# Order of two output products at the end of a segment, in a segmented-attention and GeGLU kernel

## The chip, the cores and the metric

The kernel runs on one core of one Trainium2 chip. The metric is the device time of one execution in microseconds. An engine is named by its usual letters: PE is TensorE (matmuls; PEld are its weight loads), DVE is VectorE, ACT is ScalarE, POOL is GpSimd, SP is SyncE. A DMA is issued by SP, ACT or POOL and then runs on the core's 16 DMA engines.

## The reference

Two branches work on the same `x` (2048 rows of 1024) and are mixed by a gate. Branch A is an attention over 64 segments of 32 rows with a memory of 8 rows that each segment hands to the next, so that the segments are a recurrence. Branch B is a GeGLU feed-forward network.

```
for s in range(n_seg):                      # 64 segments, one after the other
    h = concat([mem, x[s*32:(s+1)*32]])     # 40 rows
    q, k, v = h Wq, h Wk, h Wv              # 32 heads of 128
    p = softmax(where(mask, q k^T * scale, -1e9))
    o = (p v) Wo                            # 40 rows of 1024
    mem = o[:8]                             # memory of the next segment
    outs.append(o[8:])
g = sigmoid((x * gate_w).sum(-1))
b = (gelu(x w_gate) * (x w_up)) w_down
return g * concat(outs) + (1 - g) * b
```

## The kernel before

**Branch B comes first** (up to about 600 us of the span). Its product, already multiplied by (1 - g), goes to a scratch tensor `b_scr` in HBM. Gates lie in SBUF in `gseg` and `ge`.

**Then the 64 segments run, one Python iteration of `for s in range(NSEG)` each.** The weights of branch A do not all fit in SBUF. What is missing, 19 blocks of 512 KB a segment, is read again in every segment from `w_scr` into `ring`, which has room for five blocks. SP issues a block's load (L614) as soon as TensorE has used up the two ring slots that it goes into; this is the weight stream below.

**Rows of a segment.** The 8 first rows of each segment are not needed by the recurrence in the same way as the others, so four segments' first rows (4 x 8 = 32) are put together and computed once for four segments ("ext" jobs, function `ext_jobs`). The segment itself works on 24 rows of `x` and 8 rows of memory. The accumulated output of the segment stands in PSUM bank `PB[B_O]`; that of the 32 first rows in `PB[B_X]`, which is used in every fourth segment only: in the segments with `"o"` in `jobs`, s = 3, 7, 11, ... 63.

**A segment in order.** Projections q, k, q, v, k, v for two halves of the heads (`emit_P`, matmuls of line L951, into two banks that take turns, `acc`), transposes (`emit_T`, L996 and L1004), scores and softmax (`emit_S`), its transposes (`emit_PT`), the product with v (`emit_PV`, whose L1081 also writes the first rows' part into `oe`), and the output projection (`emit_O`, L1114). Ext jobs (L836 and L1097) are put between.

**The end of a segment** is the place that the change touches. ScalarE copies `PB[B_O]` to `rows` (L1338), TensorE transposes it (L1350), and VectorE copies the memory columns into `hT` (L1356). With that the next segment's first projection, q, can start. Its second one, k, writes the bank that `B_O` names, since the two banks take turns; so its first matmul waits until L1362 has read it.

- L1362, VectorE: `bo = gate * PB[B_O] + bo`, the segment's own output product. `bo` was loaded with the rows of `b_scr` (`load_b`, L734).
- L1368: four stores of `bo` to the output, on POOL's queue; in the last segment two on SP's and two on ACT's.
- `out_first` (L1146 to L1164), only where `"o"` is in `jobs`: L1154 on ScalarE scales the upper half of `PB[B_X]`, L1156 on VectorE multiplies the lower half and adds the upper, L1159 on VectorE adds branch B's rows (`rowsx`), and L1162 issues two stores from `oe`, on POOL's queue; in the last segment on SP's and ACT's.
- Behind it POOL's queue goes on with the next segment's loads of `vt` (`load_vte`, L720), of `qkst` (L708) and of `bo` (L734).

**What sets the order.** The program is written as a list of operations. Each engine runs its own in the order in which the list has them. Waits are semaphores that `_Sched` derives from the keys which an operation reads and writes (`r=`, `w=`). So where an operation stands in the list decides what it is queued behind on its engine. A PSUM bank that two engines read is read by one after the other (`_Sched.op`, L45).

The loop's end as it stands, with the functions that it calls:

Of the kernel before, what the change touches and what calls it, by code (L numbers as in the profile page):

```python
# [26 lines left out]
class _Sched:  # L27
# [10 lines left out]
    def op(self, eng, mk, r=(), w=(), dsem=None):  # L38
        o = _Op(eng, mk, dsem)
        deps = []  # L40
        if eng == "pool" and dsem is None:
            w = [*w, ("pool",)]
        for k in r:
            deps += self.w.get(k, ())
            if k[0] == "P":  # L45
                deps += [x for x in self.r.get(k, ()) if x.eng != eng]
        for k in w:
            deps += self.w.get(k, ())
            deps += self.r.get(k, ())
        for k in r:  # L50
            self.r.setdefault(k, []).append(o)
        for k in w:
            self.w[k] = [o]
            self.r[k] = []
        seen = set()
        for d in deps:
            if d is o or id(d) in seen:
                continue
            seen.add(id(d))
            if d.eng == eng and d.dsem is None and (eng == "pe" or eng == "sp"):  # L60
                continue
            o.deps.append(d)
            d.sig = True
        self.ops.append(o)
        return o
# [63 lines left out]
def bass_gated_mix__memory_aug_recurrent_mem_tr__geglu_ffn__prompt_kernel(  # L129
# [38 lines left out]
    with ExitStack() as es:  # L168
# [50 lines left out]
        def P(i):  # L219
            return ("P", i)  # L220

        g = _Sched()
        op = g.op
# [501 lines left out]
        def rows_of(s):  # L725
            n = SEG if s + 1 < NSEG else NR
            v = of[s * SEG + EXT:s * SEG + EXT + n, :]
            return [(v[:, q * 256:(q + 1) * 256], bo[32 * q:32 * q + n, :]) for q in range(4)]
# [12 lines left out]
        def first_rows(t, j, q):  # L741
            return t.rearrange("(g s r) d -> g s r d", s=GR, r=SEG)[j, :, 0:EXT, q * 512:(q + 1) * 512]
# [52 lines left out]
        for s in range(NSEG):  # L795
# [350 lines left out]
            def out_first():  # L1146
                if "o" not in jobs:
                    return
                j = jobs["o"]
                flat = [oe[z:z + 64, :, :].rearrange("p a b -> p (a b)") for z in (0, 64)]  # L1150
                sums, to = flat[0].bitcast(FP32), flat[1][:, 0:512]
                key = [("oe", y) for y in range(NO)]
                gk = [("gseg", "e%d%d" % (q, u)) for q in range(4) for u in range(GR)]
                op("act", lambda e: e.activation(sums, PB[B_X][64:128, :], ACTF.Copy, scale=ge[64:128, j:j + 1]),  # L1154
                   r=[P(B_X)] + gk, w=key)
                op("dve", lambda e: e.scalar_tensor_tensor(  # L1156
                    out=sums, in0=PB[B_X][0:64, :], scalar=ge[0:64, j:j + 1], in1=sums, op0=ALU.mult, op1=ALU.add),
                   r=[P(B_X)] + gk, w=key)
                op("dve", lambda e: e.tensor_tensor(out=to, in0=sums, in1=rowsx[0:64, :], op=ALU.add), r=RX, w=key)  # L1159
                for q in range(2):  # L1160
                    op(("sp", "act")[q] if last else "pool",
                       lambda e, q=q: e.dma_start(first_rows(of, j, q), to[32 * q:32 * q + 32, :]),  # L1162
                       r=key + [("out", x, y) for x in range(max(0, j * GR - 1), j * GR + GR - 1) for y in range(4)],
                       w=[("oute", j, q)], dsem="%s%d" % ("ende" if last else "oute", q))  # L1164
# [192 lines left out]
                back("act", ("q", 0, 4, 1), 1)  # L1357
            flush()
            last = s == NSEG - 1
            if not last:  # L1360
                out_first()
            op("dve", lambda e, s=s, B_O=B_O: e.scalar_tensor_tensor(  # L1362
                out=bo[:, :], in0=PB[B_O][:, 0:256], scalar=gseg[:, s:s + 1], in1=bo[:, :], op0=ALU.mult, op1=ALU.add),
               r=[P(B_O)] + [("gseg", "%s%d" % (k, q)) for k in "ab" for q in range(4)], w=[("bo", x) for x in range(4)])
            for put, bank in ends:
                put(bank)
            for x, (d, b) in enumerate(rows_of(s)):
                op(("sp", "act")[x % 2] if last else "pool", lambda e, d=d, b=b: e.dma_start(d, b),  # L1368
                   r=[("bo", x)], w=[("out", s, x)], dsem="%s%d" % ("end" if last else "out", x))
            if last:  # L1370
                out_first()
            if s > GR and s % GR == 2 and s // GR + 2 < NG:
                load_xe(s // GR + 2)

# [40 lines left out]
```

## Time and profile before

| what | us |
|---|---|
| median of 3 runs (2481.06 to 2482.62) | 2482.28 |
| the profiled execution | 2473.53 |
| its span, first to last instruction | 2471.4 |
| PE busy in the span | 2203.8 |
| DVE busy | 1186.5 |
| ACT busy | 940.9 |
| POOL busy | 634.9 |
| ring loads: 1216 of 512 KB, median from issue to landing | 6.3 |

The page of the profile shows one execution. Busy time is the sum of what an engine's instructions took; a chain of waits follows the end of the span back to what released it at each step; a group is all instructions of one line, engine and operation, with its busy time, the mean of one, and the idle time of the engine just before them with what ended it. A timeline lists instructions by start time. Busy times in stretches list each engine's busy time, the granted clock of TensorE, the DMA engines' busy share and what they moved. From about 645 us on, the span consists of the segments, of 27 to 33 us each.

### The profile page before, as it was taken

How to read it: one execution, taken by the hardware profiler on the slowest of the kernel's cores; microseconds unless marked ns; L12 is line 12 of the kernel's file. 1: busy time of each engine (PE TensorE's matmuls, PEld its weight loads, DVE VectorE, ACT ScalarE, POOL GpSimd, SP SyncE). 2: the span in 40 equal slices, each digit the busy share in tenths (PEclk: the TensorE clock that was granted, in tenths of full speed). 3: DMA queues.
4: the chain of work that ended last, by engine and by line, in shares of the span. 5: the costliest groups of instructions: out<-in, count | busy, mean ns of one | idle time of the engine just before them, and what ended most of it. 6: DMA issues, size and time to landing. Idle time of an engine off the chain costs nothing.

```text
span 2471.4 us, 83513 instructions
## 1 busy us (share of the span) xinstructions
PE 2203.8 (89%) x37171; PEld 1100.2 (45%) x37171; DVE 1186.5 (48%) x3451; ACT 940.9 (38%) x2212; POOL 634.9 (26%) x1132
## 2 busy tenths in 40 slices
PE   9999999999888888888888888888888888988877
PEld 4444444444444444444444444444444444444433
DVE  5626264451444455544454454455454445545444
ACT  4314132230434444444444444444444344444433
POOL 1010102102332223233323222332323232332222
PEclk9999999999999999999999999999999999999999
DMA  8727354468999999999999999999999999999998
GB/s 276 259 69 253 103 181 124 128 227 302 346 345 362 366 372 373 379 367 369 367 380 364 369 362 384 372 373 375 371 378 371 364 370 378 371 376 360 376 345 301
DMA packets 293167, 797.45 MB, mean 323 GB/s; under 512 B 48352, under 2 KB 112016, under 8 KB 292040
## 3 DMA queue, kind: packets, MB, share of 16 engines
q1 hardware_dynamic: 249308, 736.77, 80.8%
q0 software_dynamic: 43392, 55.30, 7.1%
q8 instruction: 291, 4.77, 0.8%
q14 instruction: 68, 0.56, 0.1%
q10 hardware_dynamic: 108, 0.06, 0.0%
HBM read 764.52 MB, written 37.22 MB: 324 GB/s over the span
## 4 chain that ended last, share of the span: by engine, by line
PE 54%; DMA 28%; DVE 10%; ACT 5%; issue 2%; POOL 0%; ACTq 0%; SPq 0%; DVEq 0%; POOLq 0%
DMA ring<-w_scr 27%; PE pbb L951 5%; PE pba L951 5%; PE pbc L836 5%; PE pbb L1114 3%; PE pba L1114 3%; PE pbe L1061 3%; PE pba L449 2%; PE pbd L449 2%; PE pbg L449 2%; PE pbf L449 2%; PE pbe L449 2%; PE pbh L449 2%; PE pbc L449 2%; PE pbb L449 2%
## 5 line engine op out<-in xcount | busy, mean ns | idle before, releaser
L951 PE MATMUL pbb<-arena,hT 128*32 128x512 bf16 x4416 | 337.7, 381 | 21.3 <-DVE bo L1362 21.3
L951 PE MATMUL pba<-arena,hT 128*32 128x512 bf16 x4416 | 347.8, 380 | 0.1
L720 POOL DMA_DIRECT2D vt<-v_scr x252 | 148.1, 592 | 383.4 <-PE pbf L1072 233.9
L1004 DVE COPY qk<-pbe 128x512 bf16<-128x512 bf16 x129 | 89.1, 691 | 321.9 <-PE pbe L996 315.5
L1044 ACT ACTIVATE pbd<-pbd 104x160 f32<-104x160 f32 x256 | 71.9, 281 | 437.1 <-DVE pbd L1042 437.1
L1066 DVE COPY ptb<-pbe 80x320 bf16<-80x320 bf16 x256 | 82.2, 321 | 263.3 <-PE pbe L1061 263.3
L951 PE MATMUL pba<-ring,hT 128*32 128x512 bf16 x1542 | 152.4, 384 | 34.7 <-DMA ring<-w_scr 33.3
L951 PE MATMUL pbb<-ring,hT 128*32 128x512 bf16 x1536 | 148.7, 385 | 34.9 <-DMA ring<-w_scr 33.3
L836 PE MATMUL pbc<-arena,xe 128*32 128x512 bf16 x2208 | 177.0, 385 | 0.7 <-ACT rowsx L850 0.5
L951 PEld LDWEIGHTS pbb<-arena,hT 128*32 128x32 bf16 x4416 | 109.6, 97 | 108.4 <-DVE bo L1362 28.7
L957 ACT ACTIVATE rows<-pba 128x512 bf16<-128x512 f32 x128 | 76.5, 598 | 211.0 <-PE pba L951 211.0
L1368 POOL DMA_DIRECT2D out_dram<-bo x252 | 125.8, 505 | 111.2 <-DVE bo L1362 111.0
L951 PEld LDWEIGHTS pba<-arena,hT 128*32 128x32 bf16 x4416 | 113.2, 97 | 90.8 <-issue 2.5
L957 ACT ACTIVATE rows<-pbb 128x512 bf16<-128x512 f32 x128 | 76.5, 598 | 186.8 <-PE pbb L951 186.8
L1051 DVE TENSOR_TENSOR pn<-pbd,rr 104x256 bf16<-104x256 f32 (+1 forms) x512 | 141.8, 318 | 8.7
L1061 PE MATMUL pbe<-ident,pn 104*80 104x104 bf16 x1024 | 95.5, 216 | 40.9 <-DVE pn L1051 14.2
L880 POOL DMA_DIRECT2D qk_scr<-rowsx x60 | 47.3, 789 | 329.5 <-DVE rowsx L877 329.5
L1114 PE MATMUL pba<-arena,oT 128*32 128x256 bf16 x2176 | 121.6, 281 | 10.2 <-ACT oT L1080 5.3
L1114 PE MATMUL pbb<-arena,oT 128*32 128x256 bf16 x2176 | 119.0, 277 | 11.7 <-ACT oT L1080 11.7
L1114 PE MATMUL pba<-ring,oT 128*32 128x256 bf16 x1792 | 107.0, 279 | 22.0 <-DMA ring<-w_scr 21.4
L1045 DVE TENSOR_REDUCE rs<-pbd 104x4 f32<-104x160 f32 x256 | 83.0, 324 | 88.9 <-ACT pbd L1044 88.9
L1061 PEld LDWEIGHTS pbe<-ident,pn 104*80 104x80 bf16 x1024 | 62.7, 117 | 122.8 <-issue 51.8
(262 smaller groups left out, 4369.2 us busy)
## 6 DMA issues: line engine op xcount, KB each, us to landing
ring<-w_scr SPq DMA_DIRECT2D x1216, 512.0 KB, 6.3
arena<-in_B_w_gate_dram SPq DMA_DIRECT2D x27, 1024.0 KB, 5.4
arena<-in_B_w_up_dram SPq DMA_DIRECT2D x27, 1024.0 KB, 7.8
qkst<-qk_scr POOLq DMA_DIRECT2D x126, 64.0 KB, 5.6
qk_scr<-rowsx POOLq DMA_DIRECT2D x60, 128.0 KB, 5.8
arena<-in_B_w_down_dram SPq DMA_DIRECT2D x7, 1024.0 KB, 11.8
arena<-in_A_Wk_dram SPq DMA_DIRECT2D x6, 1024.0 KB, 7.2
arena<-in_A_Wv_dram SPq DMA_DIRECT2D x6, 1024.0 KB, 10.3
```

The source lines that it names most:

```text
L449: ins = e.matmul(PB[bank][:, :], lhsT=wv[:, kc, col:col + 128], rhs=xb[:, kc, :], start=(kc == 0), stop=(kc == KC - 1))
L720: op("pool", lambda e: e.dma_start(vt[2 * SEG:KEYS, par, :], v_scr[s // GR, h, 2 * par:2 * par + 2, s % GR, :, :]), r=[("vscr", s // GR, h ...
L836: ins = e.matmul(PB[B_X][32 * gq:32 * gq + 32, :], lhsT=xe[:, us[-1], :], rhs=us[gq // 2][0][gq % 2], start=(n == 0), stop=(n == KC - 1), ...
L951: ins = e.matmul(PB[bank][32 * gq:32 * gq + 32, :], lhsT=hT[:, kc, :], rhs=us[gq // 2][0][gq % 2], start=(x == 0), stop=(x == KC - 1), ski ...
L957: op("act", lambda e: e.activation(rows[:, :], PB[bank][:, :], ACTF.Copy), r=[P(bank)], w=[("rows",)])
L1004: op("dve", lambda e: e.tensor_copy(qk[:, m, :, 0:SEG, :], src), r=[P(B_T)], w=[("qk", m)])
L1045: op("dve", lambda e: e.tensor_reduce(rsv, sv, AX.X, ALU.add), r=[P(B_S)], w=[("rs",)])
L1051: op("dve", lambda e, c0=c0, k0=k0, n=n: e.tensor_tensor(out=pn[0:104, :, c0:c0 + 2 * n].rearrange("p i (two c) -> p i two c", two=2), in0 ...
L1061: ins = e.transpose(PBV[B_PT][0:KEYS, 512 + i * 128:512 + i * 128 + 104], pn[0:104, i, :], ident[0:104, 0:104])
L1066: op("dve", lambda e: e.tensor_copy(ptb[0:KEYS, :, :, :], src), r=[P(B_PT)], w=[("ptb",)] + first)
L1114: ins = e.matmul(PB[B_O][32 * q:32 * q + 32, 0:256], lhsT=oT[:, o % 2, k, :], rhs=u[q // 2][:, (q % 2) * 256:(q % 2 + 1) * 256], start=(o ...
L1368: op(("sp", "act")[x % 2] if last else "pool", lambda e, d=d, b=b: e.dma_start(d, b), r=[("bo", x)], w=[("out", s, x)], dsem="%s%d" % ("en ...
```

## The change

The own product L1362 now comes right behind the memory copy in every segment, and `out_first` comes behind the own stores L1368 in every segment (in the last segment it stood there already). In the last segment all four own stores are issued by SP instead of two by SP and two by ACT; the two of `out_first` stay on SP and ACT.

```diff
             last = s == NSEG - 1
-            if not last:
-                out_first()
             op("dve", lambda e, s=s, B_O=B_O: e.scalar_tensor_tensor(
                 out=bo[:, :], in0=PB[B_O][:, 0:256], scalar=gseg[:, s:s + 1], in1=bo[:, :], op0=ALU.mult, op1=ALU.add),
                r=[P(B_O)] + [("gseg", "%s%d" % (k, q)) for k in "ab" for q in range(4)], w=[("bo", x) for x in range(4)])
             for put, bank in ends:
                 put(bank)
             for x, (d, b) in enumerate(rows_of(s)):
-                op(("sp", "act")[x % 2] if last else "pool", lambda e, d=d, b=b: e.dma_start(d, b),
+                op("sp" if last else "pool", lambda e, d=d, b=b: e.dma_start(d, b),
                    r=[("bo", x)], w=[("out", s, x)], dsem="%s%d" % ("end" if last else "out", x))
-            if last:
-                out_first()
+            out_first()
             if s > GR and s % GR == 2 and s // GR + 2 < NG:
                 load_xe(s // GR + 2)
```

## The prediction, made before the changed kernel ran

> **What bounds the kernel now.** I read the chain of waits first. It says which resource keeps ending last over the whole span:
>
> ```profile
> PE 54%; DMA 28%; DVE 10%; ACT 5%; issue 2%; POOL 0%; ACTq 0%; SPq 0%; DVEq 0%; POOLq 0%
> ```
>
> Nearly all of the DMA share is one transfer, the weight blocks of 512 KB that SP loads into `ring` (27% of the span). So TensorE and the weight stream share the bound: TensorE runs until the next block has not landed, and a block is only issued when TensorE has freed two slots. Next come the costliest groups, for the place that the change touches:
>
> ```profile
> L951 PE MATMUL pbb<-arena,hT 128*32 128x512 bf16 x4416 | 337.7, 381 | 21.3 <-DVE bo L1362 21.3
> ```
>
> TensorE stands idle for 21.3 us in front of projection matmuls until VectorE's L1362 has read the output bank. The view of line L1362 counts 15 such waits, so 1.42 us each. Fifteen is the number of segments with `"o"` in `jobs` that are not the last (3, 7, ... 59). The timeline around the end of segment 11, one of them, shows why (start, duration, engine, line):
>
> ```profile
> 965.87 0.19 DVE L1356 COPY hT<-pbe 128x64 bf16<-128x64 bf16 x1 [2.04 <-PE pbe L1350]
> 966.69 0.68 ACT L1154 ACTIVATE oe<-pbc,gseg 64x512 f32<-64x512 f32 x1
> 967.41 0.74 DVE L1156 SCALAR_TENSOR_TENSOR oe<-pbc,gseg,oe 64x512 f32<-64x512 f32 x1 [1.35 <-ACT oe L1154]
> 968.28 0.69 DVE L1159 TENSOR_TENSOR oe<-oe,rowsx 64x512 bf16<-64x512 f32 x1
> 969.00 0.48 DVE L1362 SCALAR_TENSOR_TENSOR bo<-pbb,gseg,bo 128x256 bf16<-128x256 f32 x1
> 969.54 0.61 PE L951 MATMUL pbb<-arena,hT 128*32 128x512 bf16 x8 [1.52 <-DVE bo L1362]
> ```
>
> The memory copy L1356 ends at 966.06 and the next segment's q projection starts. VectorE then idles 1.35 us for ScalarE's L1154, does L1156 and L1159, and only then L1362, whose bank the k projection needs. At an ordinary boundary, the one of segment 12, nothing lies between the two:
>
> ```profile
> 995.29 0.19 DVE L1356 COPY hT<-pbe 128x64 bf16<-128x64 bf16 x1 [0.51 <-PE pbe L1350]
> 995.39 0.48 DVE L1362 SCALAR_TENSOR_TENSOR bo<-pba,gseg,bo 128x256 bf16<-128x256 f32 x1
> ```
>
> Last I read busy times in stretches, because the stall can only be won if the weight stream keeps up. These are the first 10 us behind the memory copy in segments 12 to 15; segment 12 has the stall. Columns: stretch, length, busy us of PE, PEld, DVE, ACT, POOL, granted clock, DMA share, GB/s.
>
> ```profile
> 966.10:976.10 10.00, 7.98 (x164) 3.63 (x164) 4.94 (x12) 3.29 (x7) 4.95 (x9) 1.00 0.96 325
> 995.50:1005.50 10.00, 9.58 (x200) 4.60 (x204) 2.95 (x8) 3.12 (x7) 3.74 (x7) 1.00 1.03 395
> 1023.10:1033.10 10.00, 9.32 (x196) 4.36 (x196) 2.81 (x9) 2.52 (x6) 4.06 (x8) 1.00 1.00 364
> 1051.80:1061.80 10.00, 8.09 (x160) 3.52 (x160) 3.01 (x8) 2.63 (x6) 4.85 (x9) 1.00 1.03 393
> ```
>
> The same four as whole segments:
>
> ```profile
> 966.10:995.50 29.40, 24.76 (x536) 12.69 (x536) 15.30 (x50) 12.73 (x31) 9.08 (x16) 1.00 0.98 355
> 995.50:1023.10 27.60, 24.53 (x536) 12.71 (x536) 13.71 (x48) 11.91 (x30) 7.95 (x14) 1.00 1.01 383
> 1023.10:1051.80 28.70, 25.44 (x552) 12.96 (x552) 14.67 (x53) 12.16 (x30) 8.16 (x14) 1.00 1.00 378
> 1051.80:1080.40 28.60, 24.96 (x520) 12.63 (x520) 12.94 (x43) 11.11 (x28) 9.45 (x17) 1.00 1.02 382
> ```
>
> A stalled segment is longer (over segments 4 to 62 the time from copy to copy averages 29.6 us, against 28.4, 28.6 and 28.8 for the three that follow it) though TensorE works no more, and the DMA engines move fewer bytes a second in it.
>
> **The change, part by part.**
>
> 1. L1362 moves ahead of `out_first` (15 boundaries). Its inputs are there: ScalarE's read of the same bank (L1338) precedes the transposes that feed L1356. So it starts at the copy's end, as at ordinary boundaries, and ends 0.5 us later instead of 3.4 us. It fits into VectorE's 1.35 us of idle time before L1156, so L1156 and L1159 stay where they are, ending 2.9 us behind the copy. If that idle time were gone, they would be 0.48 us later, and behind them the copy L1004 of the next q rows. That one starts 4.8 us behind the memory copy now (970.86) and would be wanted at about 3.3, so it has 0.4 us to spare and pays nothing. ScalarE's order does not change at these boundaries.
>
> 2. TensorE: the eight q steps end 1.95 us behind the copy, after the bank is free. The wait goes whole: at most 15 x 1.42 = 21.3 us.
>
> 3. How much of it the ring takes back. No row shows a first-rows boundary without the stall, so I bound it. Upper end: the whole 1.42 us. Lower end: segment 15, 10 us behind its copy, has no stall and still only 8.09 us of matmuls against 7.98 in stalled segment 12, with the same sort of work; it waits for blocks instead. Adding up TensorE's idle time ahead of `ring` matmuls gives 2.5 us in a segment of its kind and 1.1 in a stalled one, and 1.1 + 1.42 is 2.5 too: a gain of 0. Against that end: a stalled segment moves 29.4 x 355 = 10.4 MB, others 10.6 to 10.9 MB. At the other three's 381 GB/s it would be done in 27.4 us, 2.0 us sooner, so the stream has room for the whole stall. And part of its slow 325 GB/s is the stall's own doing: blocks whose slots the k projection frees are issued 1.5 us late and leave a hole. Segments of segment 14's kind wait 1.4 us for blocks on average; with that the stalled one would gain 1.42 + 1.1 - 1.4 = 1.1. I take **0.85 us**, between the midpoint 0.71 and 1.1: 15 x 0.85 = 12.75 us.
>
> By the Trainium skill (DMA: Bandwidth & Descriptors, Specifications) a core's share of HBM bandwidth is about 358 GB/s; a kernel already there could gain nothing from a shorter TensorE wait, and the sum would be 0.5 us. The trace does not agree with it as a ceiling: it has 395 GB/s for 10 us and whole slices at 384.
>
> 4. POOL's queue: the four stores of `bo` now come ahead of the two of `oe`. POOL issues a store in 0.50 us (4 in 2.02) and one of `oe` in 0.59. The stores go out 0.7 to 2.7 us behind the copy instead of 4.4 to 6.4, as at ordinary boundaries. Those of `oe` wait for L1159 (2.9) and go at about 3.2, as before. Behind them stand the two `vt` loads (L720), which gain some 2 us. The next writer of `oe`, L1081, and the next load of `bo`, L734, come over 9 us behind the copy, after the landing (5.4 and 4.5 us): cost 0. Without that cover each would cost its lateness to the part of the landing still open. The collision of these stores with the ring is a rival below.
>
> 5. The last segment. Here L1362 is already first; ScalarE's share of the stores goes to SP:
>
> ```profile
> 2462.23 0.75 SPq L1368 DMA_DIRECT2D out_dram<-bo  x2
> 2462.23 1.00 ACTq L1368 DMA_DIRECT2D out_dram<-bo  x2
> 2463.28 0.68 ACT L1154 ACTIVATE oe<-pbc,gseg 64x512 f32<-64x512 f32 x1 [2.62 <-PE pbc L1097]
> ```
>
> L1154 stands behind ScalarE's two issues; TensorE finished its bank at 2462.74. Without them it starts at about 2462.8, and L1156, L1159 and the last stores follow: **0.5 us**, once. SP issues 4 x 0.375 = 1.5 us, to 2463.7; its store of `oe` is due at 2465.1, so SP costs nothing. Without that cover, 0.75 us.
>
> Sum: 12.75 + 0.5 = 13.3 us. Against the profiled execution (2473.53 us, span 2471.4) that is 2460.2 and 2458.1. The median of the runs, 2482.28, lies 8.75 us above that execution; I take the gain from the median: **2469.0 us**. 0.2% of it, about what a measurement can tell from no change, is 5 us.
>
> **Rivals.**
> - **Whole stall won.** For: the stream's room of 2.0 us, the missing hole. Against: segment 15. 2482.3 - 21.3 - 0.5 = **2460.5 us**.
> - **The ring takes it all.** For: DMA shares of 0.96 to 1.03 everywhere, segment 15's first 10 us. Against: the bytes. Gain 0 to 0.3 a boundary: **2478 to 2482 us**.
> - **Slower: the earlier stores of `bo` collide with the blocks of the k and q projections.** At present they go out while TensorE has just been idle; after the change they go out 0.7 to 2.7 us behind the copy, when these blocks are in flight and TensorE runs without pause. At boundaries that have this now, ring waits reach 3.2 us in the worst segment. The price is the growth of ring waits over 1.1 us, and it decides from 1.42 us of growth on. At 3.2 the net is 3.2 - 1.1 - 1.42 = 0.7 us: 2482.3 + 15 x 0.7 - 0.5 = **2492 us**. Against: the stalled segment has the least other traffic.
> - That the change doesn't do what it says (L1362 held by something else, as at the one boundary of 15 where a late block already hides 1 us of the stall): no row speaks for it; it counts with the second.
>
> **How the numbers follow.** Forecast 0.53 (gain 5 to 18 us); whole stall 0.23; ring takes all 0.14; slower 0.10. Faster by over 0.2%: 0.53 + 0.23 + 0.03 of the second = 0.79; within 0.2%: 0.12; slower: 0.09. The likeliest's own range is 2464 to 2477. The range reaches to 2459 (the whole stall and a little of the hole) and to 2480, inside the second rival; outside lie the slower case, 0.1, and some 0.08 of the edges.
>
> **What would show it.** Right: L1362 ends 0.5 us behind L1356 at all boundaries; no TensorE wait on L1362; idle time ahead of `ring` matmuls grows by 15 x 0.57 = 8.5 us; the first 10 us of the 15 segments rise from about 8.0 us of matmuls and 325 GB/s to 360 or more; L1154 of the last segment starts 0.5 us behind its bank. Wrong: ring waits that grow by 20 us or more, a new wait of L1004 or of POOL's `vt` loads, or segments that follow growing longer by what these 15 lose.

## The result, and the profile after

The changed kernel takes 2459.39 us (median of 4 runs, 2455.58 to 2462.47); the kernel before takes 2482.09 us beside it. The ratio is 0.9908, with a 95% interval of 0.9891 to 0.9925: 22.7 us faster. The time lies in the stated range, but near its lower edge. Two repetitions further down give a smaller gain, 11 and 15 us.

The profiled execution of the changed kernel took 2462.47 us, 11.1 us less than the one of before, and its span is 2460.7 us. Its chain of waits, by engine and, the larger shares, by line:

```profile
PE 52%; DMA 32%; DVE 9%; ACT 4%; issue 2%; POOL 0%; SPq 0%; DVEq 0%; another core or an unknown queue 0%; POOLq 0%
DMA ring<-w_scr 30%; PE pba L951 6%; PE pbb L951 5%; PE pbc L836 5%; PE pbb L1114 3%; PE pba L1114 2%; PE pbe L1061 2%; PE pbg L449 2%; PE pbh L449 2%; PE pbf L449 2%; PE pbe L449 2%; PE pbe L996 2%; PE pba L449 2%; PE pbc L449 2%; PE pbd L449 2%
```

The weight stream's share rose from 27% to 30%. Of the costliest groups, the one that had 21.3 us of idle time before it, and two of the matmuls that read streamed blocks (busy us, mean ns, idle us and what ended it):

```profile
L951 PE MATMUL pbb<-arena,hT 128*32 128x512 bf16 x4416 | 339.9, 383 | 0.0
L951 PE MATMUL pba<-ring,hT 128*32 128x512 bf16 x1542 | 152.9, 385 | 36.5 <-DMA ring<-w_scr 35.3
L951 PE MATMUL pbb<-ring,hT 128*32 128x512 bf16 x1536 | 151.4, 387 | 36.7 <-DMA ring<-w_scr 35.1
```

The wait for the own product is gone entirely. The waits for blocks in the two lower groups were 33.3 us each before. The timeline at the end of segment 11, the boundary that the prediction showed (the own product is now L1360, its stores are L1366):

```profile
960.46 0.19 DVE L1356 COPY hT<-pbe 128x64 bf16<-128x64 bf16 x1 [2.04 <-PE pbe L1350]
960.57 0.48 DVE L1360 SCALAR_TENSOR_TENSOR bo<-pbb,gseg,bo 128x256 bf16<-128x256 f32 x1
962.00 0.74 DVE L1156 SCALAR_TENSOR_TENSOR oe<-pbc,gseg,oe 64x512 f32<-64x512 f32 x1 [0.96 <-ACT oe L1154]
962.88 0.69 DVE L1159 TENSOR_TENSOR oe<-oe,rowsx 64x512 bf16<-64x512 f32 x1
```

VectorE's order is the new one, and L1159 still ends 2.9 us behind the copy. TensorE and POOL in the same stretch:

```profile
962.44 0.60 PE L951 MATMUL pbb<-arena,hT 128*32 128x512 bf16 x8
962.88 0.91 PE L951 MATMUL pbb<-ring,hT 128*32 128x512 bf16 x8
...
961.34 2.01 POOL L1366 DMA_DIRECT2D out_dram<-bo  x4 [6.45 <-DVE bo L1360]
...
963.86 1.21 POOL L1162 DMA_DIRECT2D out_dram<-oe  x2 [0.52 <-DVE oe L1159]
...
965.06 1.14 POOL L720 DMA_DIRECT2D vt<-v_scr  x2
```

The k projection starts 1.8 us behind the copy (960.65) without a pause. It then meets its second streamed block: eight matmuls of `ring` take 0.91 us where they took 0.60. The `vt` loads go out 4.4 us behind the copy, 2 us sooner than before. The busy times of segment 12 in stretches, as in the prediction:

```profile
960.60:970.60 10.00, 8.71 (x176) 3.99 (x180) 5.60 (x15) 3.39 (x7) 4.92 (x9) 1.00 0.98 362
960.60:989.30 28.70, 25.06 (x536) 12.63 (x536) 15.20 (x51) 12.89 (x31) 9.05 (x16) 1.00 1.00 367
```

In the first 10 us, 0.73 us more of matmuls than before and 362 GB/s instead of 325; the segment is 28.7 us long instead of 29.4.

### The profile page after: what moved, and what is told of

Its sections match the earlier page's. It is cut to its first block, busy times and chain, and to the rows that moved or that the text cites. A ratio compares the mean times of both kernels' runs of the same rounds, so it can differ in the third digit from the quotient of the medians.

```text
span 2460.7 us, 83457 instructions
## 1 busy us (share of the span) xinstructions
PE 2204.1 (90%) x37115; PEld 1100.5 (45%) x37171; DVE 1185.1 (48%) x3451; ACT 941.3 (38%) x2212; POOL 634.8 (26%) x1132
## 4 chain that ended last, share of the span: by engine, by line
PE 52%; DMA 32%; DVE 9%; ACT 4%; issue 2%; POOL 0%; SPq 0%; DVEq 0%; another core or an unknown queue 0%; POOLq 0%
DMA ring<-w_scr 30%; PE pba L951 6%; PE pbb L951 5%; PE pbc L836 5%; PE pbb L1114 3%; PE pba L1114 2%; PE pbe L1061 2%; PE pbg L449 2%; PE pbh L449 2%; PE pbf L449 2%; PE pbe L449 2%; PE pbe L996 2%; PE pba L449 2%; PE pbc L449 2%; PE pbd L449 2%
## 5 line engine op out<-in xcount | busy, mean ns | idle before, releaser
L1366 POOL DMA_DIRECT2D out_dram<-bo x252 | 125.6, 506 | 224.2 <-DVE bo L1360 214.6
L1114 PE MATMUL pbb<-ring,oT 128*32 128x256 bf16 x1792 | 106.3, 277 | 14.8 <-DMA ring<-w_scr 14.5
```

The costliest lines, as they stand in the source:

```text
L1114: ins = e.matmul(PB[B_O][32 * q:32 * q + 32, 0:256], lhsT=oT[:, o % 2, k, :], rhs=u[q // 2][:, (q % 2) * 256:(q % 2 + 1) * 256], start=(o ...
L1366: op("sp" if last else "pool", lambda e, d=d, b=b: e.dma_start(d, b), r=[("bo", x)], w=[("out", s, x)], dsem="%s%d" % ("end" if last else ...
```

## The experiments

All were timed in five rounds beside the kernel before on the same chip.

**The two kernels again, and each part alone.** `before_again` and `after_again` are the two kernels as they stand. `bounds_only` is the changed kernel with the last segment's stores on SP and ACT as before; `last_only` is the kernel before with only those stores moved (`...` stands for the rest of a line):

```diff
-                op("sp" if last else "pool", lambda e, d=d, b=b: e.dma_start(d, b),       # bounds_only, from after
+                op(("sp", "act")[x % 2] if last else "pool", lambda e, d=d, b=b: e.dma_start(d, b),
-                op(("sp", "act")[x % 2] if last else "pool", lambda e, d=d, b=b: ...      # last_only, from before
+                op("sp" if last else "pool", lambda e, d=d, b=b: ...
```

> The kernel before, once more, as a measure of what two programs with the same text differ by, and for a second profile of it. Both theories: ratio to the kernel before 1.000, within 0.002. The second profile again has 15 waits of TensorE on L1362, 21 us in all.

> The changed kernel, once more. Theory A (forecast: the ring takes back some 0.57 us of each stall of 1.42 us): ratio 0.9947, 13 us faster. Theory B (the whole stall of 21.3 us is won, and 0.5 us at the end): ratio 0.9912, 22 us faster. If the ratio falls near 0.9955, as the two profiled executions have it (2473.53 and 2462.47 us), the first four timed runs overstated it.

> The own product first at the 15 boundaries; the last segment's stores stay on SP and ACT. Theory A: 12.8 us faster (0.9949). Theory B: 21.3 us faster (0.9914). Rival: much of the gain comes from the last segment, then this one lies over 2 us behind the changed kernel.

> Only the last segment's four stores on SP. Theories A and B: L1154 starts 0.5 us sooner behind TensorE, 0.5 us faster, which times cannot tell from no change (0.999 to 1.001). Rival: over 2 us faster.

| kernel | median us | ratio to before (2475.08 us) | 95% interval |
|---|---|---|---|
| before_again | 2473.18 | 0.9997 | 0.9969 to 1.0025 |
| after_again | 2460.69 | 0.9939 | 0.9911 to 0.9968 |
| bounds_only | 2465.84 | 0.9955 | 0.9928 to 0.9981 |
| last_only | 2473.41 | 0.9984 | 0.9960 to 1.0008 |

The gain of `after_again` is 15 us by its ratio (14.4 by the medians), between theory A and the first result and nearer to A. Its interval, 8 to 22 us, still holds theory B's 0.9912; that of `bounds_only` doesn't. `bounds_only` lies 5 us behind `after_again`, and over 2 us was my sign for a gain that comes from the last segment. The times can't settle that: the two intervals overlap, and `last_only` can't be told from no change. The timeline does: here is ScalarE's L1154 in `last_only`. In the kernel before it idled 2.62 us and started 0.5 us later.

```profile
2465.74 1.56 SPq L1368 DMA_DIRECT2D out_dram<-bo  x4
2466.30 0.69 ACT L1154 ACTIVATE oe<-pbc,gseg 64x512 f32<-64x512 f32 x1 [2.13 <-PE pbc L1097]
2468.61 0.75 SPq L1162 DMA_DIRECT2D out_dram<-oe  x1
```

From L1362's start to L1154's it is now 1.08 us instead of 1.56, as the prediction had it, and SP's four issues end 1.3 us before its next one. From L1362's start to the end of the span it is 9.69 us in the profile of before, 9.67 in that of `bounds_only`, and 9.18 in those of `last_only` and of the changed kernel. So the last segment gives 0.5 us and not 5, and the rest of the gain is at the 15 boundaries. A third time the changed kernel was run later, for the size:

> The changed kernel a third time, for the size of the gain. Theory A: 0.9935 to 0.996 (10 to 16 us). Theory B: 0.991 (22 us), as in the first four runs.

2460.42 us against 2471.79, ratio 0.9954 (0.9933 to 0.9976): 11 us, theory A. So the changed kernel's median hardly moves (2459.4, 2460.7, 2460.4), and what moved is the kernel before. Its four runs in the first comparison lay between 2481.1 and 2482.6; its 85 runs in the four later ones lie between 2460.0 and 2493.9, with medians of 2471.8 to 2476.4. The 24 runs of the two repetitions and these 85, taken together though they are from several chips, have means 14.2 us apart (about 3.5 either way): the forecast's 13.3 lies inside, the whole stall's 21.8 outside. Of the 85, 19 lie at 2481 us or above, so four such runs in a row are rare by chance alone; what held them there is not known. Because they lie close together, the first interval came out narrower than the spread of this kernel allows.

**Is it the ring that takes part of the gain?** In both kernels, every streamed block from the fifth segment on is cut to its first half (`half_...`) or its first three quarters (`three_quarter_...`, with 768 for 512):

```diff
+            if s >= 4:
+                op("sp", lambda e: e.dma_start(ring[:, sl:sl + wd, :].rearrange("p a b -> p (a b)")[:, 0:wd * 512], src[:, 0:wd * 512]),
+                   r=[("rp", u)], w=[("ring", y, x) for y in slots for x in range(2)], dsem=f"ring{sl}")
+                return
```

> The kernel before with every ring block from the fifth segment on cut to its first half (256 KB of 512 KB; the rest of the slot keeps older weights, so the output is another one). The weight stream no longer limits: nearly no waits of TensorE on ring blocks. The waits on L1362 stay, 15 of 1.5 us. Both theories: faster than the kernel before by its ring waits, some 1.5 us a segment, 60 to 100 us (0.96 to 0.975).

> The changed kernel with the same half blocks. With the ring out of the way, the gain over the half-block kernel before is the whole stall: 15 x 1.5 = 22 us. Theory A (the ring takes back some 40% in the kernel as it is): 22 us here against 13 to 15 there. Theory B (nothing is taken back): 22 us here and there. Rival C (the gain is limited by something other than the ring, VectorE or the later segments): here too only 13 to 15 us.

> The kernel before with ring blocks of 384 KB instead of 512 KB from the fifth segment on (the last quarter of each slot keeps older weights, so the output is another one). Theory A: ring waits mostly gone; some 20 us over the half-block kernel before at most: 2373 to 2395 us.

> The changed kernel with the same blocks of 384 KB. Theory A: what the ring takes back falls with the stream, so the gain over the three-quarter kernel before lies between the 13 to 15 us of the full stream and the 25.5 us of the half one, nearer the upper end: 20 to 25 us. Theory B: 25 us at every width. Rival C (the difference between 25.5 and 13 to 15 us is chance): no order, anything from 13 to 25.

`half_before` came out at 0.9586, a little faster than expected (0.96 to 0.975), `three_quarter_before` inside its range. The pairs:

| blocks | before's order, us | changed order, us | gain, us | ring wait per stalled segment, before and after |
|---|---|---|---|---|
| 512 KB (after_again, after_third) | 2475.08, 2471.79 | 2460.69, 2460.42 | 14.4, 11.4 | 1.1 and 1.5 |
| 384 KB | 2390.99 | 2379.52 | 11.5 | 0.06 and 0.65 |
| 256 KB | 2372.54 | 2347.06 | 25.5 | 0.00 and 0.01 |

The last column is the idle time of TensorE ahead of matmuls that read streamed blocks, averaged over the segments that follow a first-rows boundary, in one profile of each kernel. With full blocks it varies: 1.0 to 1.5 in three profiles of before's order, 1.4 to 1.7 in five of the changed one. The groups of the half-block pair, first before's order and then the changed one, show the whole stall going and nothing coming back:

```profile
L955 PE MATMUL pbb<-arena,hT 128*32 128x512 bf16 x4416 | 339.0, 383 | 22.9 <-DVE bo L1366 22.9
L955 PE MATMUL pbb<-ring,hT 128*32 128x512 bf16 x1536 | 147.7, 383 | 1.8 <-DMA ring<-w_scr 1.7
```

```profile
L955 PE MATMUL pbb<-arena,hT 128*32 128x512 bf16 x4416 | 338.2, 382 | 0.0
L955 PE MATMUL pbb<-ring,hT 128*32 128x512 bf16 x1536 | 147.3, 382 | 2.1 <-DMA ring<-w_scr 2.1
```

With the ring out of the way the change is worth 25.5 us, the 22.9 us of waits and a little more. That speaks for theory A: the whole stall comes off when the ring doesn't limit. Rival C, something other than the ring, falls. My expectation for three quarters was a miss: 11.5 us, not 20 to 25. The same groups of that pair, in the same order, show where it went:

```profile
L955 PE MATMUL pbb<-arena,hT 128*32 128x512 bf16 x4416 | 338.7, 382 | 22.9 <-DVE bo L1366 22.9
L955 PE MATMUL pbb<-ring,hT 128*32 128x512 bf16 x1536 | 147.7, 382 | 11.7 <-DMA ring<-w_scr 11.2
```

```profile
L955 PE MATMUL pbb<-arena,hT 128*32 128x512 bf16 x4416 | 339.2, 383 | 0.0
L955 PE MATMUL pbb<-ring,hT 128*32 128x512 bf16 x1536 | 148.2, 383 | 19.2 <-DMA ring<-w_scr 18.9
```

Before the change these segments had almost no ring waits (0.06 us), and after it 0.65. So the waits are not there because the stream as a whole is too slow; over 900 to 2200 us its DMA share (last column but one) is 0.91 in the 384 KB kernel of before, where it is 1.00 with full blocks and 0.69 with half:

```profile
900.00:2200.00 1300.00, 1156.15 (x25416) 610.83 (x25408) 669.75 (x2241) 567.21 (x1359) 413.12 (x725) 1.00 0.91 299
```

Nor is it full just there: in the 8 us behind the memory copy of these segments the share is 0.82 before the change and 0.85 after it. The waits come from single blocks. Following each block of the full-stream kernels through the trace (issue on SP, landing, first matmul that reads it; us behind the memory copy, mean over the segments 4, 8, ... 56) gives:

```
                       before                        after
block               issue   land   use   wait    issue   land   use   wait
3  (k, second)      -3.17   3.11   4.16  0.00    -3.20   2.96   3.00  0.38
4  (q, first)       -1.18   4.37   5.68  0.00    -1.17   4.27   4.57  0.03
5  (q, second)       0.72   6.05   6.64  0.04     0.72   5.94   5.99  0.36
6  (v, first)        1.48   7.34   8.24  0.00     1.38   7.33   7.52  0.02
7  (v, second)       4.36  10.03  10.12  0.45     2.68   9.19   9.23  0.28
11 (v, second half)  8.89  16.34  17.07  0.00     8.18  15.26  16.17  0.00
```

Blocks 3 to 6 are issued before the stall could hold anything back, so they land at the same time in both kernels, and TensorE, now 1.2 us earlier at block 3, runs into them. Block 7 is the first whose slots the stall held: it is issued 1.7 us sooner, but lands only 0.84 us sooner. From there on the segment is 0.9 us ahead. With 384 KB the waits after the change are at blocks 5, 6 and 7 (0.23, 0.11 and 0.25 us; before it 0.04 at block 7 alone), and block 7, there too issued 1.7 us sooner, lands no sooner at all (8.41 against 8.36 us). So an earlier issue isn't the whole of it: block 7 also takes longer in flight (5.75 against 3.99 us), and no run here shows why.

**What a stall costs elsewhere.** In the changed kernel, a stall is put in at the 45 ordinary boundaries (`idle` is a new buffer that nothing else uses):

```diff
+            if "o" not in jobs and s > 3:
+                for put, bank in ends:
+                    put(bank)
+                for _ in range(3 - len(ends)):
+                    op("dve", lambda e: e.tensor_reduce(idle[0:104, :], mask[0:104, None, :].to_broadcast([104, 22, L]), AX.X, ALU.max),
+                       r=[("mask",), ("hT",)], w=[("idle",)])
+                ends = []
             op("dve", lambda e, s=s, B_O=B_O: e.scalar_tensor_tensor(
```

> The changed kernel with a stall put in at the 45 ordinary boundaries from segment 4 on: up to three reductions of 0.9 us on VectorE between the memory copy and the own product (ext copies that stood behind it, first), so that L1360 ends some 3.4 us behind the copy there, as it did at first-rows boundaries. Theory A: each stall of about 1.4 us costs 0.85 to 1.0 us, 38 to 45 us over the changed kernel (0.994 + 0.017 = 1.010 of the kernel before). Theory B: each costs the whole 1.4 us, 63 us (1.019).

2507.03 us, ratio 1.0114 (1.0080 to 1.0148): 46 us over the changed kernel's medians. That is theory A's number, but not its proof, since the stalls did not come out equal:

```profile
L952 PE MATMUL pba<-arena,hT 128*32 128x512 bf16 x4416 | 351.7, 384 | 48.5 <-DVE bo L1368 47.5 <-issue 0.7
L952 PE MATMUL pbb<-arena,hT 128*32 128x512 bf16 x4416 | 342.8, 386 | 3.8 <-DVE bo L1368 3.4
```

TensorE waited 51 us on the own product, not 63: 1.8 us at most boundaries of two kinds and only 0.3 at those of the third. So 51 us of stalls cost some 46. In its profile the ring waits are 86.6 us, 16 less than the 103 of the changed kernel, so stalls and ring waits together explain some 35 of the 46. The rest may be the delayed VectorE's own cost; no run separates it.

**Do the earlier stores cost anything?** VectorE's order as changed, POOL's as before:

```diff
+            if not last:
+                out_first()
             for x, (d, b) in enumerate(rows_of(s)):
                 ...
-            out_first()
+            if last:
+                out_first()
```

> VectorE's order as in the changed kernel, POOL's as before: the stores of oe first, then those of bo, 2 us later than in the changed kernel. Theories A and B: as the changed kernel, within 4 us (0.994). Rival (the early stores of bo collide with ring blocks): 5 us or more faster than the changed kernel, and fewer ring waits in the first 5 us of these segments.

2462.63 us, ratio 0.9947 (0.9927 to 0.9967), as the changed kernel's 0.9939 and 0.9954. The collision falls: with the stores of `bo`, and the `vt` loads, issued where they were before the change (4.5 and 6.5 us behind the copy), nothing is won, and the ring waits in the first 5 us are not fewer (0.54 us a segment against 0.30 to 0.39 in three profiles of the changed kernel). What the order of the stores may be worth is less than these times can tell, a few microseconds; the gain is VectorE's order.

**Can the ring's part be had too?** Block 3 is the one that TensorE meets first, so the k projection takes it two steps later (one entry of the table `KORD`):

```diff
-('k', 0): (5, 2, 6, 7, 0, 1, 4, 3)
+('k', 0): (5, 2, 6, 0, 1, 7, 4, 3)
```

> The changed kernel with the second streamed block of the first k projection used two steps (about 0.45 us) later in its order. TensorE waits for that block 0.40 us a segment on average behind first-rows boundaries and 0.76 in the segments that have first rows of their own. Theory D (each block's own timing limits): these waits go and nothing comes in their place, 10 to 20 us faster than the changed kernel (0.987 to 0.991). Theory E (the weight stream's rate limits; a wait that is taken away at one block comes back at a later one): within 5 us of the changed kernel (0.993 to 0.996), ring waits in all about 100 us as before.

2459.00 us, ratio 0.9923 (0.9900 to 0.9946). The profile speaks against theory D: at block 3 the wait falls from 0.38 to 0.04 us, and at blocks 4, 5 and 7 it rises from 0.03, 0.36 and 0.28 to 0.22, 0.58 and 0.44. Ring waits over the whole span are 100.8 us (103.9, 104.6 and 100.6 in three profiles of the changed kernel). That is what theory E expected, but it does not show a limit by rate: blocks 4 to 7 land no sooner than in the changed kernel, and TensorE, if it does not wait for block 3, reaches them earlier and waits there. The times leave open whether it is a few microseconds faster: the ratio lies between the ranges of D and E, its interval reaches into both and overlaps those of the changed kernel, and its median is theirs.

## Why the prediction came out as it did

**The mechanism was right.** L1360 ends 0.4 us behind the copy at each of the 15 boundaries, the 15 waits are gone, L1156 and L1159 did not move, POOL's two loads of `vt` came 2 us sooner, and the last segment gave its 0.5 us.

**What the ring takes back was sized about right, and for a reason that I had only half.** I took 0.85 us of each 1.42. The timed gains of the two repetitions, 11 and 15 us, less 0.5, give 0.7 to 0.97 a boundary. The profiles agree: over three of each order (those of `last_only` counted with before) the segment behind a first-rows boundary shrank from 29.54 to 28.51 us, the next one grew from 28.25 to 28.57, and the other two stayed within 0.06 us; 0.72 us net. I had listed growth of the following segments as a sign against the forecast, and in these profiles a third of the saving went that way. That part isn't firm: `bounds_only` and `pool_order` have the changed order at these boundaries too, and there the next segment takes 28.24 and 28.23 us, no more than before. Ring waits grew from 93.6 to 103.0 us in the mean of the three, 9.4 where 8.5 were forecast; with those two profiles it is 7.6, and the net of the four segments 0.9 us instead of 0.72.

**One argument of that step failed: that the stream, by its bytes a second, has room for the whole stall.** The three-quarter kernel has that room, and the ring took 0.6 us of the stall all the same. Bytes a second over a stretch do not tell it. Blocks 3 to 6 had been issued before the stall held anything back, and they land when they did before (within 0.15 us), however early TensorE wants them. The other argument, of a hole behind the stall because blocks are issued late, held in part: with full blocks block 7 gained half of its 1.7 us. Whether what holds the later blocks is the stream's rate or something else stays open.

**The base was the step that failed.** I wrote that the median of the runs lies 8.75 us above the profiled execution and took the gain from the median. That gave 2469.0 us. From the profiled execution it would have been 2460.2, which is where all three medians of the changed kernel lie. Runs of this kernel spread over 34 us; the three runs shown lay within 1.6 us of each other and above the middle. The 85 later ones have a median of 2474.9 us, 7.4 under the base that I used. That the first result still fell into the range, by 0.4 us, was luck: its lower edge had been set for the whole stall and a little of the hole, while by the later runs it was the lower base, with a gain near the forecast, that put the time there.

**The rivals.** The whole stall won (2460.5 us) met the time and, in the first comparison, the gain; the repetitions and the block table speak against it for the full stream, and with half blocks it is what happens. The ring taking it all (a gain of up to 5 us) and the slower case through colliding stores are out: both repetitions' intervals begin above 5 us, and `pool_order` shows no collision.

## What to carry to other kernels

A wait that is removed gives at most what the next limit leaves, and the bound can be read per transfer: list when each load was issued, landed and was first read, and see which of them were issued before the wait held anything back, for here these did not come sooner. Ask this of single loads rather than of bandwidth over a stretch; a stream with 9% to spare still took back 0.6 us of 1.5. A load that is issued sooner need not land as much sooner either: 1.7 us became 0.84 with 512 KB and nothing with 384. And a few runs that lie close together say little about the middle of a kernel whose runs spread: compare over rounds, and let a profiled execution that stands well below the median be a warning.

## What the runs showed of the hardware

The spread of the times goes with the stream: twelve runs of the changed kernel with full blocks lie within 36 us (2443.8 to 2479.8), five with half blocks within 8 (2344.2 to 2351.8). It goes with TensorE's granted clock too: over the 85 later runs of the kernel before, the clock lies between 0.986 and 0.995, and the longer runs have the lower one (correlation -0.64). Which of them causes the other, no run shows. A block's time from issue to landing falls with its size, but not in proportion: block 3 took 6.2 us with 512 KB, 4.9 with 384 KB and 3.3 with 256 KB in the changed order.
